# The low halves of w_out by a subtraction on VectorE instead of TensorE's identities, all queues listed anew

## The chip, the cores and the metric

The kernel runs on one core of a Trainium2 chip (trn2). The metric is the device time of one execution in microseconds. Five engines take part: TensorE (PE in the profile; PEld is its weight load), VectorE (DVE), ScalarE (ACT), GpSimd (POOL) and SyncE (SP), which issues the DMAs.

## The reference

Two stages follow one another. The first is a recurrence with a complex decay, for 4 batches of 8 heads, 768 steps and a head dimension of 48; its output is the input of a gated feed-forward layer (384 to 1024 to 384) with a convolution over three steps in its gate. All data are float32, the weights are drawn as float64 and read as such.

```
mag = sqrt(a_re^2 + a_im^2);  scale = min(mag, 0.999) / (mag + 1e-6)
for t in range(768):                       # per batch and head
    S_re, S_im = complex decay of S by scale * (a_re + i a_im)[t]
    S_re += outer(k[t], v[t])
    y[t] = q[t] @ S_re
x = y, heads side by side                  # (4, 768, 384)
h = relu(x @ w_in)                         # w_in 384 x 1024
gate = sigmoid(conv3(h, conv_w))           # along the steps, per channel
out = (h * gate) @ w_out                   # w_out 1024 x 384
```

## The kernel before

**Attention.** The recurrence is done in chunks of 128 steps, two chunks to a segment, twelve segments in all. For each segment `prelude` (L295) turns the decays into running sums of logarithms and phases (squares, Ln, Exp, Arctan on ScalarE; scans on VectorE), and `products` (L334) multiplies q and k with the exponentials, sines and cosines. L351 and L352 make the two parts of k, L353 those of q. Eight DMAs for each of the two, one per head (L358), copy them into `stk` tiles with one head's rows side by side. Per chunk, `state` (L368) updates the running state on TensorE (transposes L378 copied by L379, products L385, copy L392), and `attention` (L395) does the rest: L403 multiplies the stacked parts in two groups of four heads, L406 masks them on VectorE, L416 multiplies with v and the state, and L428 (ScalarE) and L429 (VectorE) split the result into a high and a low half, `x`, for the feed-forward layer.

**Feed-forward.** It works on units of 256 or 384 steps, in steps of 256 channels (`moe_front` L469, `moe_back` L491). Each number is kept as two fp32r halves, and a product takes three matmuls: high by high, high by low, low by high. L482 is x by w_in, L485 the relu, L486 and L488 the convolution, L500 the tanh, L501 the gate, L503 and L504 the high and low half of the gated result (`hg`), L509 the product with w_out, L515 the copy before the DMA to the output.

**Weights.** `load_weights` (L264) runs for w_in and w_out, in four pairs of 128x768 each. A pair arrives as float64 in a `stk` tile (the same four buffers that the attention's copies use), `to_f32` (L241, rows L243, L244, L246) makes float32 of it on VectorE in a `g_t` tile, and L276 rounds that to the high half on ScalarE. For the low half, TensorE adds the tile by an identity (L280, two rows a matmul in the profile) and subtracts the high half by a negative identity (L281), in two cuts of 384 columns, each in a PSUM buffer `h_ps` of its own (two buffers, shared with L482); L282 copies each cut to the low half on ScalarE. The low halves are first read by L482 (w_in) and L509 (w_out).

**Order.** Nothing is left to the program's order. `in_order` (L165) takes all pieces of work as they are written, gives each the number of `RANKS` at its place, sorts by it, and makes a chain of each engine's instructions in that order. SyncE's queue is such a chain too: a DMA that waits holds up all behind it. Where a ScalarE function isn't in the table set loaded, a table load (L186) is put ahead of it, so the number of loads follows from the list as well. The list has 1759 numbers, one for each piece.

Of the kernel before, what the change touches and what calls it, by code (L numbers as in the profile page):

```python
# [11 lines left out]
F32 = mybir.dt.float32  # L12
# [3 lines left out]
ALU = mybir.AluOpType  # L16
# [178 lines left out]
def linear_attention_moe_kernel(ctx: ExitStack, tc: tile.TileContext, a, qk, v, w_in, conv_w, w_out, out):  # L195
    nc = tc.nc
# [38 lines left out]
    wo = const.tile([128, NB, 2, 2, DM], F32R, name="wo")  # L235
# [28 lines left out]
    def load_weights(w, src, t0):  # L264
        for i in range(NB):
            at_time(t0 + 4 * i)
            pair = (w[:, i].rearrange("p i f k c -> p i (f k c)") if len(w.shape) == 6 else
                    w[:, i].rearrange("p i f c -> p i (f c)"))
# [436 lines left out]
```

## Time and profile before

| | |
|---|---|
| median of three runs | 395.29 us (393.75 to 396.29) |
| the profiled execution's own time | 395.28 us |
| its span, first to last instruction | 393.5 us |
| mean granted TensorE clock | 0.994 |
| TensorE busy | 353.5 us, 90% |
| VectorE busy | 334.5 us, 85% |
| ScalarE busy | 338.8 us, 86% |
| GpSimd busy | 3.8 us, 1% |

Busy time is the time in which at least one instruction of an engine runs; neighbouring instructions overlap a little, so that the mean length of one is somewhat more than the distance from one start to the next. In a row of a timeline stand the start and length in us, the engine, the line and operation, the tile written and those read, the shape, the count of merged instructions, and in brackets the engine's idle time before it with what ended it. The execution's time is 1.8 us longer than the span.

### The profile page before, as it was taken

Reading aid. Unit: us, or ns where it says so; the run is one execution under the profiler, and the core shown is the slowest. Engines: PE = TensorE matmul, PEld = TensorE weight load, DVE = VectorE, ACT = ScalarE, POOL = GpSimd, SP = SyncE. Lnnn points to the kernel's source line nnn. Section 1 sums busy time; section 2 is a strip of 40 time slices with the busy share of each in tenths; the row PEclk is TensorE's granted clock in tenths of the full one; section 3 lists DMA queues with packets and bytes.
Section 4 is the critical chain, followed back from the end, with each engine's and each line's share of the span. In section 5 each row is a group of like instructions: output and inputs, shape, how many; then the busy total and the mean of one; then the engine's idle time right before and its main releaser. Section 6 shows DMA issues by size and latency. Waiting matters only on the chain. (4 is left out here: it accounts for less than half of the span.)

```text
span 393.5 us, 10104 instructions
## 1 busy us (share of the span) xinstructions
PE 353.5 (90%) x4146; PEld 323.6 (82%) x4146; DVE 334.5 (85%) x515; ACT 338.8 (86%) x577; POOL 3.8 (1%) x33
## 2 busy tenths in 40 slices
PE   1436678898999999999999999999999999999994
PEld 1113457788999999999999999999998999999994
DVE  3799996998999999999999987999988977773780
ACT  4999999998999999999999999999988985442641
POOL 2000000000000000000000000000000000000000
PEclk9999989999999999999999999999999999999999
DMA  8974958777853843687828636821818606500102
GB/s 301 415 269 151 146 131 150 272 123 241 133 158 107 161 143 122 127 212 164 198 33 178 201 102 135 219 77 52 138 30 149 194 15 116 95 2 2 60 2 69
DMA packets 31495, 55.03 MB, mean 140 GB/s; under 512 B 4304, under 2 KB 25808, under 8 KB 31440
## 3 DMA queue, kind: packets, MB, share of 16 engines
q1 hardware_dynamic: 31440, 54.31, 55.2%
q8 instruction: 34, 0.56, 0.6%
q14 instruction: 21, 0.17, 0.1%
HBM read 30.70 MB, written 4.72 MB: 90 GB/s over the span
## 5 line engine op out<-in xcount | busy, mean ns | idle before, releaser
L509 PE MATMUL o<-wo,hg 128*128 128x384 f32 x576 | 115.8, 345 | 0.9 <-ACT os_t L515 0.8
L482 PE MATMUL h_ps<-x,wi 128*128 128x386 f32 (+1 forms) x648 | 111.7, 324 | 0.1
L482 PEld LDWEIGHTS h_ps<-x,wi 128*128 128x128 f32 x648 | 103.5, 189 | 0.7 <-ACT h_t L485 0.4
L509 PEld LDWEIGHTS o<-wo,hg 128*128 128x128 f32 x576 | 98.1, 189 | 4.0 <-issue 1.2
L403 PE MATMUL ps<-stk 96*128 96x128 f32 x384 | 50.9, 282 | 1.3 <-DMA stk<-a_t 1.0
L403 PEld LDWEIGHTS ps<-stk 96*128 96x128 f32 x384 | 48.1, 196 | 3.6 <-issue 1.4
L186 ACT ACT_TABLE_LOAD x39 | 50.0, 1283 | 0.6
L486 DVE SCALAR_TENSOR_TENSOR g_t<-h_t,cw 128x384 f32<-128x384 f32 (+1 forms) x72 | 40.1, 568 | 8.9 <-ACT h_t L485 8.5
L280 PE MATMUL h_ps<-g_t,ident 128*128 128x384 f32 x32 | 20.0, 736 | 28.4 <-DVE g_t L246 11.7
L500 ACT ACTIVATE g_t<-g_t,cw 128x384 f32<-128x384 f32 (+1 forms) x72 | 39.8, 574 | 6.4 <-DVE g_t L488 6.1
L485 ACT ACTIVATE h_t<-h_ps 128x386 f32<-128x386 f32 (+1 forms) x72 | 31.6, 450 | 15.0 <-PE h_ps L482 15.0
L488 DVE SCALAR_TENSOR_TENSOR g_t<-h_t,cw,g_t 128x384 f32<-128x384 f32 (+1 forms) x72 | 40.1, 567 | 0.5
L406 DVE TENSOR_TENSOR p_t<-ps,mask 128x512 f32<-128x512 f32 x48 | 32.9, 686 | 7.9 <-PE ps L403 7.6
L280 PEld LDWEIGHTS h_ps<-g_t,ident 128*128 128x128 f32 x32 | 7.1, 261 | 34.9 <-issue 13.3
L504 DVE TENSOR_TENSOR hg<-g_t,hg 128x768 fp32r<-128x768 f32 (+1 forms) x36 | 31.1, 864 | 4.6 <-ACT hg L503 3.6
L503 ACT ACTIVATE hg<-g_t 128x768 fp32r<-128x768 f32 (+1 forms) x36 | 27.7, 770 | 5.6 <-PE o L509 3.7
L501 DVE SCALAR_TENSOR_TENSOR g_t<-g_t,h_t 128x768 f32<-128x768 f32 (+1 forms) x36 | 30.9, 863 | 1.9 <-ACT g_t L500 1.8
L416 PE MATMUL ps<-p_t,v_t 128*32 128x128 f32 x768 | 26.7, 273 | 0.3 <-DVE p_t L406 0.3
L416 PEld LDWEIGHTS ps<-p_t,v_t 128*32 128x32 f32 x768 | 22.1, 109 | 1.4 <-DVE p_t L406 0.5
L378 PE MATMUL ps<-ident,qk_t 128*128 128x128 f32 x120 | 20.5, 287 | 2.6 <-ACT kn L379 2.6
L416 PE MATMUL ps<-stk,s_sb 96*32 96x128 f32 x640 | 22.0, 276 | 0.0
L353 DVE TENSOR_TENSOR a_t<-a_t 128x1536 f32<-128x1536 f32 x12 | 21.0, 1752 | 0.1
(93 smaller groups left out, 482.0 us busy)
## 6 DMA issues: line engine op xcount, KB each, us to landing
a_t<-in_a SPq DMA_DIRECT2D x12, 768.0 KB, 6.1
qk_t<-in_qk SPq DMA_DIRECT2D x12, 768.0 KB, 4.5
stk<-qk_t SPq DMA_DIRECT2D x96, 96.0 KB, 3.0
stk<-a_t SPq DMA_DIRECT2D x96, 96.0 KB, 2.9
v_t<-in_v SPq DMA_DIRECT2D x12, 448.0 KB, 4.0
out<-os_t SPq DMA_DIRECT2D x24, 192.0 KB, 2.9
stk<-in_w_in SPq DMA_DIRECT2D x4, 768.0 KB, 10.5
stk<-in_w_out SPq DMA_DIRECT2D x4, 768.0 KB, 8.0
```

Source lines behind the costliest of these rows:

```text
L186: row = [nc.scalar.preload_act_table_set(min(loads[k])).ins, *row]
L403: nc.tensor.matmul(sp[:, h], lhsT=stk[0][:, hq * 4 + h], rhs=stk[1][:, hq * 4 + h], start=(h == 0), stop=(h == 3))
L406: nc.vector.tensor_tensor(out=p, in0=sp, in1=mask.unsqueeze(1).broadcast_to([128, 4, C]), op=ALU.mult)
L416: nc.tensor.matmul(yp[r0:r0 + 32, q // 4], lhsT=left[:, i, col:col + 32], rhs=right(h), start=r0 not in started, stop=n == len(sources) - ...
L482: nc.tensor.matmul(hp, lhsT=wi[:, f2, iw, i, kt], rhs=x[ix][:, kt], start=(k == 0), stop=(k == 8))
L485: nc.scalar.activation(h, hp, func=AF.Relu)
L486: nc.vector.scalar_tensor_tensor(out=g, in0=h[:, 0:n], scalar=cw[:, f, 0:1], in1=h[:, 1:n + 1], op0=ALU.mult, op1=ALU.add)
L488: nc.vector.scalar_tensor_tensor(out=g, in0=h[:, 2:n + 2], scalar=cw[:, f, 2:3], in1=g, op0=ALU.mult, op1=ALU.add)
L500: nc.scalar.activation(g[:, i], g[:, i], func=AF.Tanh, scale=cw[:, 2 * f2 + i, 1:2])
L501: nc.vector.scalar_tensor_tensor(out=g, in0=g, scalar=1.0, in1=h[:, :, 1:n + 1], op0=ALU.add, op1=ALU.mult)
L504: nc.vector.tensor_tensor(out=lo, in0=g, in1=hi.bitcast(F32), op=ALU.subtract)
L509: nc.tensor.matmul(ops[t], lhsT=hg[:, k, t * C:(t + 1) * C], rhs=wo[:, f2, w, k], start=(f2 == 0 and hg is hi and k == 0 and w == 0), stop ...
```

## The change

For w_out, the low half of a pair is now one subtraction on VectorE (L275 of the new file), float32 tile minus high half, over all 768 columns, written straight to the weight tile. The two cuts with their matmuls (L280, L281) and copies (L282) are left out there. For w_in they stay. The list of ranks is a new one with 1739 numbers, twenty fewer: six pieces of each of the four pairs of w_out go and one comes. Nearly every number in it is different, so the order on all engines and of the DMAs changes, within what the data allow. Of the 160 lines of ranks in the diff the first old and the first new one stand here.

```diff
--- before.py
+++ after.py
@@ -43,86 +43,86 @@
 RANKS = [
-    5, 7, 0, 4, 6, 11, 14, 9, 2, 10, 8, 13, 12, 3, 4, 4, 5, 6, 7, 8, 9, 10,
...
+    2, 9, 0, 10, 12, 5, 14, 1, 11, 6, 8, 13, 4, 0, 2, 3, 4, 5, 6, 7, 8, 9,
...
@@ -274,6 +274,9 @@
             tmp = mo.tile([128, 2, HT], F32, name="g_t", bufs=GBUF).rearrange("p a b -> p (a b)")[:, 0:WP]
             to_f32(tmp.bitcast(I32), raw, tmp.bitcast(I32))
             nc.scalar.activation(pair[:, 0], tmp, func=AF.Copy)
+            if w is wo:
+                nc.vector.tensor_tensor(out=pair[:, 1], in0=tmp, in1=pair[:, 0].bitcast(F32), op=ALU.subtract)
+                continue
             for c in range(2):
                 cut = slice(c * DM, (c + 1) * DM)
                 rest = psH.tile([128, 512], F32, name="h_ps")[:, 0:DM]
```

## Rows read from the trace of the kernel before

**Rows 1.** Page part 1: engine, busy us, share of the span, instructions.

```profile
PE 353.5 (90%) x4146; PEld 323.6 (82%) x4146; DVE 334.5 (85%) x515; ACT 338.8 (86%) x577; POOL 3.8 (1%) x33
```

**Rows 2.** Windows: stretch, length, busy us (count) by engine, clock, DMA share, GB/s.

```profile
60.00:70.00 10.00, 8.44 (x167) 7.43 (x169) 6.87 (x12) 9.98 (x20) 0.00 (x0) 1.00 0.88 184
...
80.00:90.00 10.00, 9.51 (x165) 8.70 (x164) 9.88 (x20) 9.97 (x19) 0.00 (x0) 1.00 0.78 117
...
100.00:120.00 20.00, 20.00 (x264) 18.66 (x263) 19.23 (x36) 19.13 (x36) 0.13 (x2) 1.00 0.64 136
```

**Rows 3.** Timeline of TensorE, 48 to 110 us.

```profile
50.49 1.43 PE L280 MATMUL h_ps<-g_t,ident 128*128 128x384 f32 x2 [2.84 <-ACT wo L282]
51.71 3.12 PE L403 MATMUL ps<-stk 96*128 96x128 f32 x16
...
59.90 0.91 PE L280 MATMUL h_ps<-g_t,ident 128*128 128x384 f32 x2
60.35 0.63 PE L281 MATMUL h_ps<-wo,minus 128*128 128x384 f32 x1
60.82 1.95 PE L403 MATMUL ps<-stk 96*128 96x128 f32 x16
...
88.55 0.88 PE L385 MATMUL s_ps<-v_t,kn 128*32 128x48 f32 x48
...
90.94 1.83 PE L403 MATMUL ps<-stk 96*128 96x128 f32 x14 [0.69 <-DMA stk<-a_t]
92.52 1.32 PE L482 MATMUL h_ps<-x,wi 128*128 128x258 f32 x9
```

**Rows 4.** Timeline of ScalarE, last 8 us.

```profile
388.07 0.49 ACT L515 ACTIVATE os_t<-o 128x384 f32<-128x384 f32 x1 [1.68 <-PEq L568]
```

**Rows 5.** Groups by line and shape: count, busy us, mean ns, idle before.

```profile
L186 ACT ACT_TABLE_LOAD x39 | 50.0, 1283 | 0.6
...
L282 ACT ACTIVATE wo<-h_ps 128x384 fp32r<-128x384 f32 x8 | 3.9, 488 | 0.0
...
L504 DVE TENSOR_TENSOR hg<-g_t,hg 128x768 fp32r<-128x768 f32 x24 | 22.9, 953 | 3.7 <-ACT hg L503 2.9 <-PE o L509 0.5
```

**Rows 6.** Timeline of ScalarE, 38 to 110 us.

```profile
58.18 0.47 ACT L282 ACTIVATE wo<-h_ps 128x384 fp32r<-128x384 f32 x1
58.55 0.93 ACT L312 ACTIVATE e_t<-e_t,inv 128x768 f32<-128x768 f32 x1
```

**Rows 7.** Timeline of VectorE, 38 to 110 us.

```profile
37.09 0.95 DVE L352 TENSOR_TENSOR qk_t<-qk_t,a_t 128x768 f32<-128x768 f32 x1
...
59.51 2.04 DVE L317 TENSOR_TENSOR_SCAN a_t<-a_t,cl,e_t 128x256 f32<-128x256 f32 x3 [0.56 <-ACT e_t L312]
...
67.01 0.56 DVE L429 TENSOR_TENSOR x<-ps,x 128x384 fp32r<-128x384 f32 x1 [1.97 <-ACT x L428]
68.32 0.96 DVE L314 TENSOR_TENSOR a_t<-a_t 128x768 f32<-128x768 f32 x1 [0.75 <-DMA stk<-a_t]
...
71.02 0.96 DVE L345 TENSOR_TENSOR a_t<-qk_t,a_t 128x768 f32<-128x768 f32 x1 [0.42 <-DMA qk_t<-in_qk]
71.90 0.95 DVE L344 TENSOR_TENSOR qk_t<-qk_t 128x768 f32<-128x768 f32 x1
...
75.86 0.93 DVE L352 TENSOR_TENSOR qk_t<-qk_t,a_t 128x768 f32<-128x768 f32 x1
```

**Rows 8.** Timeline of SyncE's queue: issues of DMAs, 0 to 110 us.

```profile
76.82 5.70 SPq L358 DMA_DIRECT2D stk<-qk_t  x8
83.05 6.23 SPq L358 DMA_DIRECT2D stk<-a_t  x8
```

**Rows 9.** Windows of TensorE alone: busy us, granted clock, DMA share, GB/s.

```profile
52.00:54.00 2.00, 2.00 (x11) 0.50 0.82 323
```

**Rows 10.** Timelines of VectorE and TensorE, 136 to 165 us.

```profile
138.65 0.69 DVE L504 TENSOR_TENSOR hg<-g_t,hg 128x512 fp32r<-128x512 f32 x1
...
149.68 0.68 PE L509 MATMUL o<-wo,hg 128*128 128x384 f32 x3
```

158 rows, old and new, of the table RANKS are left out of this document.

## The prediction

> **What bounds the kernel now.** I read the page first: TensorE has the largest share, 353.5 of 393.5 us [rows 1]. Then the windows, to see where TensorE's missing 40 us lie. From 60 to 90 us it still has gaps while ScalarE is busy 9.97 to 9.98 of every 10 us; from 100 us on TensorE is busy 20.00 of 20 (one window of eight up to 360 us stands; one of the others has a small gap) [rows 2]. So there are two regimes. Up to about 91 us ScalarE and VectorE make the attention products, convert the weights, and TensorE waits for them. After that TensorE is never short of work, though both others stay almost full. TensorE's last gap of that first stretch ends at 90.94 us, where an L403 has waited 0.69 us for a DMA into stk [rows 3]. The last copy, L515, starts at 388.07 us [rows 4], right behind the last matmul.
>
> The end is therefore a sum: the moment of the last early gap (90.9), plus TensorE's work queued behind it (388.0 - 90.9 = 297.1), plus 5.5 us of tail to the end of the span at 393.5. The profiled execution took 395.28 us, 1.8 us more than its span; the median of the three runs is 395.29, so the two need no correction. A change pays only if it moves that gap, or leaves less TensorE work behind it.
>
> **What is removed.** On TensorE: per half pair of w_out two L280 rows and one L281. The ones that start at 59.90 are followed by the next work at 60.82, so 0.92 us each [rows 3], and eight of them are 7.4 us. All lie between 40 and 61 us, before the gap, where TensorE waits for others anyway; they take nothing off the 297.1 us. I cost them at nothing directly. The cover is those waits; without it they would be worth 7.4 us.
>
> On ScalarE: eight L282 copies, 0.488 us each [rows 5]. They overlap their neighbours: the one at 58.18 is followed at 58.55 [rows 6], so 0.37 us of the engine, 3.0 us for eight. The new list also needs 38 table loads instead of 39 (found by sorting the rows by rank and following the table each function needs), 1.28 us [rows 5]; both lists have eight of them before the first h copy, so that load is saved later.
>
> **What is added.** Four subtractions on VectorE, 128x768 fp32r from two fp32 tiles in SBUF. L504 has the same shape and operation: 0.953 us [rows 5]; start to start 0.88 (an L345 of the same width at 71.02, the next at 71.90 [rows 7]). So 3.5 to 3.8 us; I take 3.5. Each waits for its L276 on ScalarE, and what queues behind it is VectorE's whole list. Behind the first stands the first segment's L352, behind the second and third the masks (L406) and splits (L429) of the first chunks, so a late L276 would hold up TensorE too. In the new list the L276 stands well ahead of its subtraction, except the second, some 3 us before.
>
> **What is moved.** All five queues are listed anew, so I compare how much work stands ahead of the same step in both lists, with start-to-start times.
>
> First segment: L352, which starts its copies into stk, has 0.5 us less VectorE work ahead of it (27.2 before, 26.8 after, the first subtraction included). ScalarE's part in front of it is also no longer. Walking both lists from the first transfer I get about 36.4 us for its start against 37.09 [rows 7]. The conversion of w_out's second pair moves back by 5.8 us of VectorE work. It frees the stk buffer for this segment's second set of copies, and everything on SP stands behind that wait: these copies start about 44 us. Their L403 could then start at about 50, still not behind the old 51.71 [rows 3], where it stood in line behind the weight matmuls. Cost nothing.
>
> Third segment (whose copies make the last gap): L352 starts at 75.86 [rows 7]. The list ahead of it grows from 60.8 to 64.1 us: three subtractions (2.6) and one scan more (0.65), 3.3 in all. Against that VectorE's own waits from 59 to 71 us are 0.56, 1.97, 0.75 and 0.42 us, together 3.7 [rows 7]. The largest is for ScalarE's L428. ScalarE's list up to the L428 of the third chunk loses eight L282, one L276 and one L392 and gains four other steps, 0.9 us less in all. An engine that comes 3.3 us later for answers that come 0.9 us earlier doesn't wait for them: the waits go, and L352 starts at 75.86 + 3.3 - 3.7 = 75.5. VectorE is then as far as before with only one subtraction to go.
>
> The last gap: the segment's 16 copies are issued one after the other, 76.82 to 89.28 us [rows 8]. The old order is all eight of qk_t, then all eight of a_t, the new one alternates in fours. So the first four heads can be multiplied after half of the issues, and the last heads land 0.4 us sooner, at about 90.5. By then the new TensorE list has done one L482 group of nine more (1.3 us), one L385 group less (0.9), and the first half of an L403 sixteen (1.0) that used to wait: 1.4 us [rows 3]. That leaves 295.7 behind the gap. Together 0.4 + 1.4 = 1.8 us, so 395.28 - 1.8 = 393.5.
>
> [...]
>
> **The rivals.** *Cold chunks.* Without the w_out matmuls TensorE has little to do from 41 to 50 us and from 57 to 60. If the second chunk then runs at the lower level, its L403 take 3.12 instead of 1.95 (+1.2) and its transposes and L416 about 0.9 more, on the path to L429 and the third L352: +2.1, 395.6. For it: the row at 0.50. Against: TensorE was sparse there before too, and its L403 at 60.82 are fast [rows 3].
>
> *ScalarE is the real bound.* It is full while the gaps last, VectorE waits for it, and at 100 us it is still busy 19.13 of 20 [rows 2]. If every microsecond off it counts, the gain is 3.0 + 1.3 = 4.3: 391.0. Against: after 91 us TensorE waits for neither.
>
> *Just too late, slower than before.* The new list puts many L504 later on VectorE. The eighth with 512 columns starts at 138.65, and the matmuls that read it follow at 149.68 [rows 10]: a reserve of 10.5 us. In the new list it has 10.4 us more VectorE work ahead (3.3 of it already made good above) and its matmuls come 3.5 us of TensorE work sooner: the reserve is about zero. If VectorE runs 1 or 2 us behind such places, each puts a gap into TensorE's full stretch, and these add up. Four gaps of 1.6 us, an estimate, give 393.5 + 6.5 = 400.0; it turns into a loss from 1.8 us of gaps on. For it: VectorE is busy 19.23 of 20 us at 100 us [rows 2]. Against: the list that is read this way is only compared, not followed; where VectorE is behind, its own waits shrink first, as above.
>
> **How the numbers follow.** The forecast, 393.5, has a chance of 0.45, cold chunks 0.15, ScalarE 0.25, too late 0.15. One per cent, 3.95 us, is about what a measurement of this kernel can tell from no change; it puts the borders at 391.3 and 399.2. The first two cases are within them: 0.60. ScalarE's is faster, 0.25, and the last slower, 0.15. For the range I leave out a little on either side: 389.5, which takes in 391.0 with the subtraction's bounds, and 399.0, which takes in the cold clock and most of the gaps.
>
> **What would show it.** L281 rows on wo gone, four subtractions of 0.95 us on VectorE; the third L352 at 75 to 76 us with VectorE's waits from 59 to 71 gone; the last early gap at about 90.5; TensorE without gaps of over 1 us from 100 us on. Wrong would be an L352 of the third segment that starts after 78 us, a clock at 0.50 past 56 us, or rows of L509 that wait for hg.

## The result, and the profile after

| | before | after |
|---|---|---|
| median | 394.74 us (8 runs) | 397.77 us (8 runs, 397.08 to 398.42) |
| ratio, 95% interval | 1 | 1.0072 [1.0054, 1.0089] |
| the profiled execution's own time | 395.28 us | 398.20 us |
| its span | 393.5 us | 396.4 us |

The changed kernel is slower, by 0.7%. That lies within 1% and within the range, but on the other side of no change than the forecast of 393.5 us. The ratio and its interval are the record's own estimate; the quotient of the two medians is 1.0077, so differences of some 0.1% between ratios are not to be read. Executions over 1.5% slower than the fastest of the same kernel are left out of all ratios and ranges here.

Behind the subtraction, which is L278 of the changed kernel (and not L275, as the section on the change has it), all line numbers are three higher: L403 is L406, L416 is L419, L352 is L355, L482 is L485, and L280 and L281, which are left for w_in, are L283 and L284.

The first part of its page, to be held against [rows 1]:

```profile
PE 350.3 (88%) x4122; PEld 323.5 (82%) x4122; DVE 337.0 (85%) x519; ACT 336.0 (85%) x568; POOL 4.0 (1%) x33
```

The change did what it says: 24 TensorE instructions fewer, four VectorE instructions more, nine on ScalarE fewer (eight copies and a table load). TensorE works 3.2 us less, and the span is 2.9 us longer. The window from 60 to 70 us, against [rows 2]:

```profile
60.00:70.00 10.00, 8.49 (x137) 7.79 (x138) 8.30 (x13) 8.75 (x15) 0.00 (x0) 0.66 0.93 194
```

TensorE is as busy there as before but with 30 instructions less, and the granted clock is 0.66 instead of 1.00. Windows of TensorE alone show how long the clock stays down (columns: stretch, length, busy us and count, granted clock, DMA share, GB/s); in the kernel before it was down from about 50.7 to 54.2 us (0.69, 0.50 and 0.96 in three windows of 2 us from 50 us on), the dip of [rows 9]:

```profile
45.00:50.00 5.00, 0.18 (x1) 0.63 0.62 107
50.00:55.00 5.00, 4.12 (x16) 0.50 0.59 118
55.00:60.00 5.00, 4.00 (x36) 0.50 0.77 185
60.00:65.00 5.00, 4.17 (x24) 0.50 0.92 154
65.00:70.00 5.00, 4.31 (x119) 0.83 0.93 233
```

TensorE did next to nothing from 43 to 50 us (0.18 us of work from 45 to 50), and the lower level, 0.50, then held from 50 to 65. Its timeline, against [rows 3]:

```profile
39.62 1.55 PE L283 MATMUL h_ps<-g_t,ident 128*128 128x384 f32 x2
...
49.82 2.26 PE L406 MATMUL ps<-stk 96*128 96x128 f32 x8 [6.70 <-DMA stk<-a_t]
52.77 2.04 PE L406 MATMUL ps<-stk 96*128 96x128 f32 x8 [0.70 <-DMA stk<-a_t]
...
61.31 3.62 PE L406 MATMUL ps<-stk 96*128 96x128 f32 x16
64.86 1.50 PE L388 MATMUL s_ps<-v_t,kn 128*32 128x48 f32 x48
...
69.94 2.36 PE L406 MATMUL ps<-stk 96*128 96x128 f32 x16
...
91.58 0.49 PE L406 MATMUL ps<-stk 96*128 96x128 f32 x2
92.72 0.94 PE L406 MATMUL ps<-stk 96*128 96x128 f32 x6 [0.65 <-DMA stk<-qk_t]
93.89 1.13 PE L406 MATMUL ps<-stk 96*128 96x128 f32 x8 [0.24 <-DMA stk<-a_t]
...
102.30 1.94 PE L485 MATMUL h_ps<-x,wi 128*128 128x258 f32 x14 [0.46 <-ACT h_t L488]
```

The weight matmuls that stood between 42 and 52 us are gone, and one wait of 6.70 us stands there. The second chunk's sixteen L406 take 3.62 us, where they took 1.95. The last early gap ends at 93.89 us, not at 90.94, and at 102.30 us there is a gap where the kernel before had none. VectorE in the stretch of [rows 7]:

```profile
37.28 0.95 DVE L355 TENSOR_TENSOR qk_t<-qk_t,a_t 128x768 f32<-128x768 f32 x1
...
60.80 0.95 DVE L278 TENSOR_TENSOR wo<-g_t,wo 128x768 fp32r<-128x768 f32 x1
...
63.26 0.69 DVE L409 TENSOR_TENSOR p_t<-ps,mask 128x512 f32<-128x512 f32 x1 [0.64 <-PE ps L406]
...
64.96 0.69 DVE L409 TENSOR_TENSOR p_t<-ps,mask 128x512 f32<-128x512 f32 x1 [0.36 <-PE ps L406]
...
71.04 0.69 DVE L409 TENSOR_TENSOR p_t<-ps,mask 128x512 f32<-128x512 f32 x1 [1.50 <-PE ps L406]
...
78.18 0.93 DVE L355 TENSOR_TENSOR qk_t<-qk_t,a_t 128x768 f32<-128x768 f32 x1
```

The subtraction is L278, 0.95 us as costed. The waits for ScalarE are gone but for 0.17 and 0.22 us, as forecast, but waits for TensorE's scores have come in their place (0.64, 0.36 and 1.50 us). Two of the three signs of being wrong that the prediction named have come: the third segment's L355 starts at 78.18, past 78, and the clock is at 0.50 past 56 us. SyncE's queue, against [rows 8]:

```profile
45.57 5.05 SPq L361 DMA_DIRECT2D stk<-a_t  x8
...
79.14 3.22 SPq L361 DMA_DIRECT2D stk<-qk_t  x4
...
89.25 2.29 SPq L361 DMA_DIRECT2D stk<-a_t  x2
```

The third segment's copies take 12.4 us of issues as before, and start 2.3 us later. The last copy of the output, against [rows 4]:

```profile
390.73 0.49 ACT L518 ACTIVATE os_t<-o 128x384 f32<-128x384 f32 x1 [1.64 <-PEq L571]
```

So in the terms of the prediction: the gap at 93.9 (forecast 90.5), 296.8 us of TensorE behind it up to 390.7 (forecast 295.7), and a tail of 5.7.

### The profile page after: what moved, and what is told of

Read it like the earlier page. It is cut to its first block, busy times and chain, and to the rows that moved or that the text cites. A ratio compares the mean times of both kernels' runs of the same rounds, so it can differ in the third digit from the quotient of the medians.

```text
span 396.4 us, 10058 instructions
## 1 busy us (share of the span) xinstructions
PE 350.3 (88%) x4122; PEld 323.5 (82%) x4122; DVE 337.0 (85%) x519; ACT 336.0 (85%) x568; POOL 4.0 (1%) x33
## 5 line engine op out<-in xcount | busy, mean ns | idle before, releaser
L512 PE MATMUL o<-wo,hg 128*128 128x384 f32 x576 | 115.6, 345 | 0.0
L485 PE MATMUL h_ps<-x,wi 128*128 128x386 f32 (+1 forms) x648 | 111.3, 324 | 0.5 <-ACT h_t L488 0.5
L485 PEld LDWEIGHTS h_ps<-x,wi 128*128 128x128 f32 x648 | 103.5, 189 | 2.0 <-ACT h_t L488 1.0
L512 PEld LDWEIGHTS o<-wo,hg 128*128 128x128 f32 x576 | 97.6, 188 | 2.2 <-issue 0.8
L406 PE MATMUL ps<-stk 96*128 96x128 f32 x384 | 54.9, 292 | 8.5 <-DMA stk<-a_t 7.6
L406 PEld LDWEIGHTS ps<-stk 96*128 96x128 f32 x384 | 50.5, 203 | 11.3 <-issue 8.0
L283 PE MATMUL h_ps<-g_t,ident 128*128 128x384 f32 x16 | 11.4, 851 | 21.5 <-DVE g_t L246 13.6
L381 PE MATMUL ps<-ident,qk_t 128*128 128x128 f32 x120 | 21.3, 295 | 9.6 <-DVE qk_t L355 5.1
L419 PE MATMUL ps<-p_t,v_t 128*32 128x128 f32 x768 | 27.9, 279 | 0.3 <-DVE p_t L409 0.3
L381 PEld LDWEIGHTS ps<-ident,qk_t 128*128 128x128 f32 x120 | 14.7, 148 | 14.8 <-DVE qk_t L355 5.9
L283 PEld LDWEIGHTS h_ps<-g_t,ident 128*128 128x128 f32 x16 | 4.3, 306 | 24.8 <-issue 15.2
L419 PEld LDWEIGHTS ps<-p_t,v_t 128*32 128x32 f32 x768 | 22.8, 111 | 2.0 <-DVE p_t L409 1.0
L419 PE MATMUL ps<-stk,s_sb 96*32 96x128 f32 x640 | 22.3, 278 | 0.0
## 6 DMA issues: line engine op xcount, KB each, us to landing
stk<-in_w_out SPq DMA_DIRECT2D x4, 768.0 KB, 10.5
```

The source lines that it names most:

```text
L381: nc.tensor.transpose(tr[:, g - lo], kv[:, g // NG, g % NG], ident)
L406: nc.tensor.matmul(sp[:, h], lhsT=stk[0][:, hq * 4 + h], rhs=stk[1][:, hq * 4 + h], start=(h == 0), stop=(h == 3))
L419: nc.tensor.matmul(yp[r0:r0 + 32, q // 4], lhsT=left[:, i, col:col + 32], rhs=right(h), start=r0 not in started, stop=n == len(sources) - ...
L485: nc.tensor.matmul(hp, lhsT=wi[:, f2, iw, i, kt], rhs=x[ix][:, kt], start=(k == 0), stop=(k == 8))
L512: nc.tensor.matmul(ops[t], lhsT=hg[:, k, t * C:(t + 1) * C], rhs=wo[:, f2, w, k], start=(f2 == 0 and hg is hi and k == 0 and w == 0), stop ...
```

## The experiments

All ratios are to the kernel before, run beside it on the same chip, with 95% intervals. Two kinds of edit are used. One is the list: the new one, or the old one with the pieces of w_out left out or added. The other is matmuls whose result nobody reads; where a kernel has them, they are one 128x128 product of the identity with itself each (two rows in the profile), put at given places of TensorE's order:

```diff
+    def warm():
+        for k, (_, n) in enumerate(WARM):
...
+            junk = psO.tile([128, DM], F32, name="o2")
+            for _ in range(n):
+                nc.tensor.matmul(junk[:, 0:128], lhsT=ident, rhs=ident, start=True, stop=True)
```

On the new list the function moves the lines behind it by 13 more: L403 of the kernel before is L419 there, L416 is L432, L378 is L394, and the unread ones are L298.

| list | w_out's low halves | unread matmuls | ratio, 95% interval |
|---|---|---|---|
| new | subtraction (the change) | none | 1.0072 [1.0054, 1.0089]; again 1.0061 [1.0039, 1.0083] |
| new | subtraction | 28 identities, 33 to 60 us | 1.0042 [1.0021, 1.0063] |
| new | subtraction | 44, same places | 1.0016 [0.9998, 1.0033]; again 1.0007 [0.9991, 1.0024] |
| new | subtraction | 27, all before 32 us | 1.0055 [1.0035, 1.0075] |
| old | subtraction | none | 1.0104 [1.0079, 1.0129] |
| old | subtraction | w_out's own 24 kept | 1.0009 [0.9997, 1.0021] |
| old | subtraction | 37 identities | 1.0030 [1.0013, 1.0047] |
| old | subtraction | w_out's 24 and 21 identities | 0.9990 [0.9971, 1.0009] |
| old | by TensorE (before) | 21 identities | 0.9983 [0.9967, 1.0000] |
| old | none, zero | w_out's 24 kept | 0.9988 [0.9971, 1.0004] |

**The change with the old list**, and **the same with w_out's matmuls kept.** These two show what the matmuls did. In the expectations, the clock theory is that the missing matmuls cost time through TensorE's granted clock; the order theory, that the new list does; the VectorE theory, that the four subtractions do. The first is the change without its new list (the four subtractions stand where VectorE used to wait):

```diff
-RANKS = [ (the new list)
+RANKS = [ (the old list; w_out's L280, L281 and L282 left out, the subtractions at 50.5, 69.5, 72.5 and 76.5 of VectorE)
```

> The change with the old list: w_out's matmuls and copies dropped from it, the four subtractions put where VectorE used to wait; all else in the old order. Clock theory: TensorE is as empty as in the changed kernel, so 396.5 to 398.5. Order theory: the loss was the new list's, so 394.0 to 395.0. VectorE theory (four subtractions are too much before the first gap): 396 to 398 with the clock at 1.00.

The second has the subtraction too, but TensorE still makes its own low halves, and no one copies them:

```diff
+            if w is wo:
+                nc.vector.tensor_tensor(out=pair[:, 1], in0=tmp, in1=pair[:, 0].bitcast(F32), op=ALU.subtract)
...
-                nc.scalar.activation(pair[:, 1, cut], rest, func=AF.Copy)
+                if w is not wo:
+                    nc.scalar.activation(pair[:, 1, cut], rest, func=AF.Copy)
```

> As the one with the old list, but w_out's 24 matmul rows stay on TensorE at their old places, with nobody reading them; the low half comes from the subtraction, ScalarE's eight copies are gone. Clock theory: the clock is as before the change, and what is left is 3.0 us off ScalarE: 393.0 to 394.7. Order theory: the same as the one without the matmuls, within 0.5. VectorE theory: 396 to 398.

Measured: 399.16 us, 1.0104, and 395.76 us, 1.0009. The two kernels differ by 24 matmul rows whose result nobody reads, and the one that has more work to do is faster by 3.4 us. That rules out the order theory, which expected no difference. Both times lie above the clock theory's own ranges, by 0.7 and 1.1 us: more is lost without the matmuls than it said, and ScalarE's 3.0 us are not gained. TensorE's timeline of the first:

```profile
54.75 2.96 PE L419 MATMUL ps<-p_t,v_t 128*32 128x128 f32 x32 [2.25 <-DVE p_t L409]
...
59.83 3.68 PE L406 MATMUL ps<-stk 96*128 96x128 f32 x16
63.44 1.50 PE L388 MATMUL s_ps<-v_t,kn 128*32 128x48 f32 x48
...
77.48 3.66 PE L485 MATMUL h_ps<-x,wi 128*128 128x258 f32 x18
...
97.34 1.16 PE L406 MATMUL ps<-stk 96*128 96x128 f32 x8
```

and of the second (L283 is w_out's L281 there):

```profile
54.90 2.96 PE L419 MATMUL ps<-p_t,v_t 128*32 128x128 f32 x32 [2.78 <-DVE p_t L409]
...
61.23 0.63 PE L283 MATMUL h_ps<-wo,minus 128*128 128x384 f32 x1
61.70 1.95 PE L406 MATMUL ps<-stk 96*128 96x128 f32 x16
63.58 0.88 PE L388 MATMUL s_ps<-v_t,kn 128*32 128x48 f32 x48
...
95.82 1.16 PE L406 MATMUL ps<-stk 96*128 96x128 f32 x8
```

Both run the first chunk's L419 at the lower level, after a wait of over 2 us: 2.96 us at a granted clock of 0.50 from 55 to 60 us, where the second chunk's take 1.08 in the second kernel. Then the first has 0.59 us of waiting and few instructions, and its second chunk is slow; the second has w_out's matmuls from 58.56 to 61.70, and its second chunk runs at the higher level (0.98 from 60 to 65 us, 0.50 in the first): 1.95 for 3.68 us, 0.88 for 1.50. In the first the clock is down again, at 0.60 from 76 to 80 us, where eighteen L485 take 3.66 us; they take 2.41 in the second, at 1.00.

By 97 us the first is 1.5 us behind (97.34 against 95.82 at the same instruction). The rest of the 3.5 us between these two executions comes later: the distance is 1.6 us at 223 us and 3.3 at 243. ScalarE's row in the first:

```profile
229.06 0.49 ACT L518 ACTIVATE os_t<-o 128x384 f32<-128x384 f32 x1 [1.63 <-DMA out<-os_t]
```

It waits for an output DMA to leave the tile that it writes; the second kernel has no such wait there. That this wait follows from the missing matmuls is not shown.

**The new list with unread identities.** 28 of them (12 before the first transposes, 13 before the first chunk's scores, 3 between the chunks), and then 44 (12, 26 and 6) at the same places.

> The changed kernel with its list, and 28 matmuls of 128x128 by the identity added on TensorE alone, in its empty stretches (12 ahead of the first transposes, 13 ahead of the first L403, 3 between the first chunks); nothing reads them. [...] Order or VectorE theory (the new list, or the four subtractions, make VectorE late whatever the clock): 397 to 398.5.

> The changed kernel with more of the idle matmuls by the identity (12, 26 and 6 in the same three places), so that TensorE works on from 41 to 47 us instead of 45. With the first warm kernel the clock fell to 0.50 at 50 us, after a gap of 5.1 us, and the first two chunks were still slow. Clock theory: the clock now stays at 1.00 through most of 40 to 66 us, the last early gap comes at 90 to 91 us, 394.5 to 396 us. If the first warm kernel already gave back all that the clock costs: 396.5 again, and what is left is the new list's own, in its gaps after 100 us.

Measured: 396.65 us, 1.0042, between the clock theory's 394 to 395.5 us and the other theory's range, and 395.62 us, 1.0016, as the clock theory expected. TensorE and VectorE with 44 of them:

```profile
41.52 6.07 PE L298 MATMUL o<-ident 128*128 128x128 f32 x52
...
58.69 1.50 PE L298 MATMUL o<-ident 128*128 128x128 f32 x12
...
60.81 1.06 PE L419 MATMUL ps<-stk 96*128 96x128 f32 x8
62.38 1.16 PE L419 MATMUL ps<-stk 96*128 96x128 f32 x8 [0.51 <-ACT kn L395]
...
91.41 1.13 PE L419 MATMUL ps<-stk 96*128 96x128 f32 x8 [0.60 <-DMA stk<-a_t]
```

```profile
69.54 0.69 DVE L422 TENSOR_TENSOR p_t<-ps,mask 128x512 f32<-128x512 f32 x1 [1.55 <-PE ps L419]
...
76.53 0.93 DVE L368 TENSOR_TENSOR qk_t<-qk_t,a_t 128x768 f32<-128x768 f32 x1
```

The second chunk's scores are at the higher level (1.06 and 1.16 us for eight, granted 1.00 from 60 to 65 us), the third segment's L352 (L368 here) is at 76.53 instead of 78.18, the last early gap ends at 91.41 instead of 93.89, and the last copy starts at 387.27 instead of 390.73. Nothing but work that nobody reads was added. The wait for the third chunk's scores is still there (1.55 us), so it is not the clock's.

With 28 the second chunk is as fast (1.06 and 1.16 us), L352 starts at 76.57, and the gap ends no later than with 44:

```profile
91.05 2.10 PE L419 MATMUL ps<-stk 96*128 96x128 f32 x16 [0.57 <-DVE x L445]
```

What sets the two profiled executions apart (396.29 and 394.67 us) lies behind the gap, where TensorE waits 1.6 us with 28 and 0.6 with 44. The clock in the early chunks does not explain the difference between 28 and 44, and their intervals overlap.

**The same number of identities at another place.** A shift of the program could have done it too, so 27 of them were put before 32 us (10, 12 and 5, in three waits for w_in), and the changed kernel and the kernel with 44 were run again beside it.

> The changed kernel itself, unaltered, beside the others of this job. Theory and rival alike: 1.005 to 1.009, as before (1.0072); it is the mark that the next three are read against.

> The changed kernel with 27 unread identity matmuls, about as many as in the run that gave 1.0042, but all before 32 us, where TensorE waits for the conversion of w_in (10, 12 and 5 of them in three waits), so that a wait of some 5 us follows before the first transposes. Theory (what counts is the clock at the chunks from 50 to 67 us): no gain there, L403 of the second chunk again at 0.22 to 0.25 us each, time within 0.2% of the changed kernel beside it. Rival (any added TensorE instructions shift the program and bring the gain): as the run with 28, 0.3% below the changed kernel.

> The run that gave 1.0016 (12, 26 and 6 identity matmuls), unaltered, on the chip of this job beside the changed kernel. Theory: 0.4 to 0.7% below the changed kernel, 1.000 to 1.003. Rival (the chip made the difference between it and the run with 70): 1.005, no better than the run with 70 of them.

Measured: the changed kernel 1.0061, with 27 before 32 us 1.0055 [1.0035, 1.0075], with 44 in the chunks 1.0007. So these 27, at that place, give nothing back in time. TensorE of the middle one:

```profile
49.83 2.35 PE L419 MATMUL ps<-stk 96*128 96x128 f32 x8 [6.98 <-DMA stk<-a_t]
...
61.12 1.06 PE L419 MATMUL ps<-stk 96*128 96x128 f32 x8
62.69 2.08 PE L419 MATMUL ps<-stk 96*128 96x128 f32 x8 [0.51 <-ACT kn L395]
```

The expectation was met in time, and only in part in the rows: half of the second chunk's scores ran at the higher level (1.06 us for eight), the other half at the lower (2.08), with a mean of 0.77 granted from 60 to 65 us. Its last early gap ends at 92.12 us, 1.8 us before the changed kernel's, but TensorE then waits 3.4 us behind it in this execution, which takes that back. So the place counts in time; in the rows it is not a clean case.

The profiled execution of the kernel with 44 took 398.12 us this time, 2.1 us above that kernel's median. Its second chunk is fast, but the third is not:

```profile
69.95 2.50 PE L419 MATMUL ps<-stk 96*128 96x128 f32 x10 [0.64 <-DMA stk<-a_t]
```

The granted clock is 0.66 from 70 to 75 us, L352 starts at 78.73, and the last early gap ends at 93.89 us, as in the changed kernel. With not one instruction changed, an execution in which a chunk is cold, and a copy late, is as slow as the changed kernel.

**The old list with identities, and the kernel before with them.** 37 in the places of w_out's matmuls; and 21 added to the kernel before (8 at 32 us, 10 at 48, 3 behind the first chunk's scores).

> The change with the old list and w_out's matmuls gone, and 37 idle matmuls by the identity in TensorE's empty stretches (8, 18, 8 and 3). Clock theory: it is the clock, and not anything else about the dropped matmuls, that cost 3.4 us against the kernel that kept them; so back to 395 to 396. If the dropped matmuls mattered in another way (their waits held later work apart): 398 to 399.5 as without the idle matmuls.

> The kernel before with 21 idle matmuls by the identity at the two places where its own clock was down or TensorE idle ahead of the first L403 (8 at 32 us, 10 at 48 us, 3 after the first chunk's L403). Clock theory: the one stretch at 0.50 (from 51 us) goes or gets shorter; since VectorE hardly waited for those L403 (0.2 us), 394.5 to 395.5 against 395.57, at best 1 us. If the clock of these chunks is on the path there too: 393.5 to 394.5.

Measured: 396.96 us, 1.0030, so by the ratios 2.9 of the 4.1 us that the change costs on the old list come back, where the clock theory expected nearly all of it; in the profiled execution the clock is not all the way up either (0.77 to 0.88 in the windows from 40 to 60 us). And 394.64 us, 0.9983, within the first of its two ranges. In the kernel before with them the clock is 1.00 in every window from 40 to 80 us; two of them:

```profile
50.00:55.00 5.00, 4.22 (x40) 1.00 0.66 179
55.00:60.00 5.00, 3.38 (x28) 1.00 0.68 96
```

The interval touches 1: about 0.7 us may be had there, more was not found.

**The old list with both.** The subtraction, w_out's matmuls unread, and the 21 identities: an attempt to take TensorE's clock out of the comparison.

> The old list with the low halves of w_out by subtraction, w_out's 24 rows of matmuls kept on TensorE and not read, and 21 unread identity matmuls more, at the places where they took the kernel before to a clock of 1.00 throughout (8 at 32 us, 10 at 48, 3 behind the first chunk's L403). The kernel before with them gave 0.9983, this one without them 1.0009. Theory (at an equal clock the exchange of eight copies on ScalarE for four subtractions on VectorE costs or gives next to nothing): 0.997 to 1.000. Rival (the subtractions themselves cost): 1.001 or more at a clock of 1.00.

Measured: 395.32 us, 0.9990, beside 0.9983 for the kernel before with the same identities, measured apart. The clock is not quite equal: it is 0.66 from 55 to 60 us here, 1.00 in the other windows from 40 to 80 us, and 1.00 in all of them there; from 60 to 65 us, the stretch of the second chunk's scores, it is 1.00 in both. So at a nearly equal clock the exchange of eight copies on ScalarE for four subtractions on VectorE gives nothing that can be measured.

**ScalarE's copies alone.** The old list, w_out's low halves left out of the result (zeroed once by GpSimd), their matmuls kept and unread: no L282 on w_out, and no subtraction either.

```diff
+    for i in range(NB):
+        nc.gpsimd.memset(wo[:, i, 1].bitcast(F32), 0.0)
...
-                nc.scalar.activation(pair[:, 1, cut], rest, func=AF.Copy)
+                if w is not wo:
+                    nc.scalar.activation(pair[:, 1, cut], rest, func=AF.Copy)
```

> The kernel before without any low half of w_out: the 24 matmul rows stay and nothing reads them, the eight copies on ScalarE are gone, no subtraction is made, and the low half is set to zero once by GpSimd. So w_out's low half is left out of the result. It measures ScalarE's 3.0 us alone, at an unchanged clock. ScalarE theory: 392 to 393.5. VectorE theory (the subtractions take back what the copies give): 393 to 394. If the path before the gap is VectorE's and TensorE's alone: 395 to 396, as with the subtractions.

Measured: 394.78 us, 0.9988 [0.9971, 1.0004], in none of the three ranges and nearest to the last. ScalarE's 3.0 us alone give 0.5 us, and the interval includes nothing at all. Against the kernel with the subtraction and otherwise the same (1.0009 [0.9997, 1.0021], measured apart), the four subtractions cost 0.21%, some 0.8 us of their 3.5; the two intervals overlap, so this too may be nothing.

**w_out's second pair converted early.** In the new list its conversion frees the stk buffer on which the first segment's second set of copies waits; here it stands right behind the first L353.

```diff
-    15, 16, 43, 12, 34, 36, 38, 34, 42, 13, 49, 50, 52, 62, 72, 14, ...
+    15, 16, 43, 12, 34, 36, 38, 34, 42, 13, 46.2, 46.4, 46.6, 62, 72, 14, ...
```

> The changed kernel with one move in its list: the three conversions of w_out's second pair stand right behind the first L353 and ahead of two scans, so that the stk buffer comes free about 2 us sooner. Buffer theory (the first L403 waits 6.7 us for copies into that buffer, and that is what is lost): 395.5 to 396.5. Clock theory: the wait is not on the path, 397.3 to 398.3.

Measured: 398.84 us, 1.0090 [1.0065, 1.0115], 0.5 us above the clock theory's range and far from the buffer theory's. The copies did come earlier, and with them the first scores, but nothing behind them:

```profile
48.87 2.05 PE L406 MATMUL ps<-stk 96*128 96x128 f32 x8 [6.07 <-DMA stk<-a_t]
...
56.41 2.96 PE L419 MATMUL ps<-p_t,v_t 128*32 128x128 f32 x32 [3.06 <-DVE p_t L409]
```

An earlier buffer alone gives nothing back. The test is not a clean one: the same move brings VectorE later to the masks, and L419 starts at 56.41 instead of 55.13.

**More identities, and one stretch alone.** 70 of them (12, 42, 10 and 6), 58 (the same without the first 12), the first 12 alone, and 56 (12, 34, 4 and 6).

> The changed kernel with 70 unread identity matmuls on TensorE: 12 before the first transposes, 42 behind them up to the first L403 (so that the wait from 47.6 to 49.8 us is filled too), 10 between the two halves of the first chunk's L403, 6 between the chunks. The runs with 28 and 44 of them gave 1.0042 and 1.0016, with the clock at 0.50 for 10 and for 6 us after 52 us. Theory (the lost matmuls cost through the clock): clock 1.00 from 40 us on, the L403 behind the second wait at 0.12 us each instead of 0.25, the last early gap at 89 to 90 us, time 0.996 to 1.001 of the kernel before. Rival (a remainder belongs to the change or to the new list, not to the clock): the clock is up and the ratio stays at 1.0016 or above.

> The changed kernel with only the 12 unread identity matmuls before the first transposes (33 to 38 us). It tells at which of the two cold stretches the time is lost. If the first one (cold L283 and L284 at 38 to 42 us, for which ScalarE waited 1.2 us) counts: gain of about 1 us on the changed kernel, 1.0045. If all is lost in the chunks from 50 to 67 us: 1.007 as without them, with the clock back at 0.50 from 46 us on.

> The changed kernel with only the unread identity matmuls from 41 us on (42, 10 and 6 of them), and none before the first transposes. If the loss lies in the chunks from 50 to 67 us: 1.000 to 1.003. If the first stretch counts for as much: about 1.004.

> The changed kernel with 12, 34, 4 and 6 identity matmuls: the wait before the first chunk's L403 filled up to about 49.3 us, but not past the landing of the first copies at 49.8. Theory: the first chunk's L403 not delayed and at 0.12 us each, last early gap at 89 to 90 us, 0.998 to 1.002, and 0.5 to 0.9% below the changed kernel. Rival (beyond about 40 of them the unread matmuls cost more than the clock returns): 1.003 or more.

Measured: 1.0050 [1.0025, 1.0076] with 70, 1.0048 [1.0022, 1.0074] with 58, 1.0055 [1.0029, 1.0081] with 12, 1.0026 [0.9997, 1.0055] with 56. The 12 alone, which the first cold stretch before 42 us (0.50 from 38 to 42 us in the changed kernel) was to answer to, give 0.1 to 0.2%, within the intervals. The others miss their expectation: beyond 44 nothing more is gained, although the kernel with 56 has its clock at 1.00 in every window from 40 to 75 us. That speaks against the clock as the whole of the loss, or for a cost of the added matmuls; no run parts the two. Their executions scatter more: 395.6 to 400.6 us with 70, 394.6 to 400.2 with 56. In the profiled one with 56, TensorE lost 1.30 us at 126.3, right behind a wait of ScalarE of 2.17 us for the input DMA of a_t (up to 124.45), and 1.44 us at 97.7 where the trace shows nothing that it waited for. Why that happens in some executions is open.

## Why the prediction was wrong

**The step that failed** is the one on w_out's matmuls: "they take nothing off the 297.1 us. I cost them at nothing directly", with the waits as the cover. They were costed as work to be hidden, and as work no run shows a cost of them (1.0009 with them kept unread). What they also did shows in TensorE's granted clock: on the old list it is 0.98 from 60 to 65 us with them and 0.50 without. In the changed kernel it stayed at 0.50 from 50 to 65 us, and the second chunk's matmuls stand on the path to the third segment's L352. The pair of kernels on the old list, which differ in these matmuls alone, puts the loss of them at 399.16 - 395.76 = 3.4 us; on the new list unread matmuls in the same stretch give back 2.2 us (1.0072 to 1.0016; the second time 2.1, 1.0061 to 1.0007). That the missing matmuls cost this is shown. How much of it is the clock of the early chunks is shown only in part: by the traces it is 2.5 us at the last early gap on the new list (93.89 to 91.41), and 1.5 us by 97 us on the old one. What is lost later, in waits that differ from execution to execution, is not traced to it.

The rows show it too: sixteen score matmuls take 1.95 us behind w_out's matmuls and 3.62 to 3.68 us without them. By what rule the granted clock falls and rises is not shown; the runs show where it did.

**The rival was right, its size and chance were not.** Cold chunks had 395.6 us and a chance of 0.15; measured were 397.77 us. Its lower level is the granted 0.50 of [rows 9]. The row that spoke against it, sixteen L403 in 1.95 us at 60.82 [rows 3], was itself the work of the w_out matmuls from 57 to 61 us, which the change removes: the row had to be read with what stood ahead of it. The prediction's +1.2 for the scores became 3.62 - 1.95 = 1.7; its 0.9 for transposes and L416, an estimate that names no row, became 0.8 and 0.3 (1.11 and 0.69 us for 0.66 and 0.38, 1.37 for 1.08); L388 cost 0.6 more (1.50 for 0.88), and the stretch from the second chunk's scores to the third's is 8.63 us long (61.31 to 69.94), with 44 identities 7.23 (60.81 to 68.04), and 6.96 in the kernel before (60.82 to 67.78).

**First and third segment.** The first L352 was forecast at 36.4 and came at 37.28, as late as before, and its second set of copies came at 45.57 for about 44. The third was forecast at 75.5 and came at 78.18. VectorE's waits of [rows 7] did go, but 0.64 and 0.36 us for the second chunk's cold scores came, and 1.50 us for the third chunk's, which also stands there with the clock up (1.55 us, with 44 identities): a new wait of the new list, which the prediction's "the waits go" did not see. With the clock up the third L352 is at 76.53: 1.65 of the miss go with the clock (1.00 from 60 to 65 us, for 0.50), and 1.0 is the count of VectorE's work and waits in the new list, too hopeful by that.

**The last gap.** With the alternating copies the scores of the first four heads were done before the gap, as foreseen, and the 16 copies take 12.4 us to issue as before. The gap came at 93.89 for 90.5; all but 0.7 us of that is the later L352.

**The work behind it.** Forecast 295.7, measured 390.7 - 93.9 = 296.8, against 297.1. Of this, 1.4 us are gaps behind 100 us: 0.46 (102.30), 0.51 (126.85) and 0.40 (221.07), the last two waits for VectorE's L432; the kernel before has 0.85 there. Less work is queued, and new waits take most of it. Ahead of both waits for L432 stands one for a DMA, on ScalarE and on VectorE:

```profile
124.98 0.85 ACT L307 ACTIVATE a_t<-a_t 128x768 f32<-128x768 f32 x1 [1.37 <-DMA a_t<-in_a]
...
218.53 0.96 DVE L347 TENSOR_TENSOR qk_t<-qk_t 128x768 f32<-128x768 f32 x1 [0.85 <-DMA stk<-qk_t]
```

So the rival of being *just too late*, a VectorE with too much work ahead of it, is not what these rows show; the gaps are 1.4 us instead of the 6.5 it was given, and no L512 waits for hg. They are not the same each time: another profiled execution of the changed kernel, at 400.63 us, waits 2.52 us at 222.21, behind a wait of VectorE's L347 of 2.98 us for a DMA.

**ScalarE is the real bound** is refuted for the copies: their 3.0 us alone give 0.9988 [0.9971, 1.0004], some 1.1 us at the most by the interval.

**Right** were the subtraction's 0.95 us, most of its cover (0.8 of 3.5 us show in the time, within the intervals), the one table load less (38 for 39), though no run times it alone, and that the exchange as such is worth under 1% either way. That the later stk buffer costs nothing was not tested cleanly. The new list is no loss: without the matmuls it stands at 1.0072 and 1.0061, the old one at 1.0104. Three slips in the prediction's figures move nothing: 27.2 to 26.8 is 0.4 us and not 0.5, the reserve in [rows 10] is 10.3 us and not 10.5, and ScalarE is busy 9.96 us from 70 to 80 us.

## What to carry to other kernels

A matmul in a wait can be free as work and still matter to the next one on the path: here sixteen scores took 1.95 us behind w_out's matmuls, at a granted clock of 0.98, and 3.68 us without them, at 0.50 (the pair on the old list, from 60 to 65 us). Before taking such a matmul out, read the granted clock and the durations of what follows it, and ask what stood ahead of each fast row. Where a change of this kind is slower than it should be, put the removed matmuls back unread: a single kernel then tells whether their result or their mere presence counted, and the durations behind them tell whether it was the clock. And stop at the number that keeps the next critical products fast; more of them gave nothing here. A profile is one execution: compare its time with the median before reading a difference of one or two us out of it.

## What was not expected of the hardware

The granted clock of the record is not enough to find slow matmuls. In the kernel before it stands at 1.00 from 28 to 32 us, while two L280 rows take 1.65 us; at 41.97 they take 0.91. The windows, and the timeline, of TensorE in the kernel before:

```profile
28.00:32.00 4.00, 3.72 (x6) 1.00 0.75 217
40.00:44.00 4.00, 3.22 (x56) 1.00 0.93 151
```

```profile
29.89 1.65 PE L280 MATMUL h_ps<-g_t,ident 128*128 128x384 f32 x2 [0.20 <-ACT wi L282]
...
41.97 0.91 PE L280 MATMUL h_ps<-g_t,ident 128*128 128x384 f32 x2
```

Two other kernels show the same: four rows of such matmuls at 35.6 to 35.7 us take 2.93 us in both kernels of the pair on the old list, with a recorded clock of 0.54 from 30 to 40 us in the one without w_out's matmuls and 1.00 in the other. So the mean clock of an execution doesn't sort kernels: the changed kernel on the old list took 399.4 us in executions with a recorded mean of 0.967 and of 0.999. The durations of equal matmuls, 1.65 against 0.91 us at the same recorded 1.00, show a difference that the record does not.
